# First transform stage with x as weights, and its result turned by DMA transposes inside SBUF

## The chip, the cores and the metric

The kernel runs on one core of one Trainium2 chip. The metric is the device time of one execution in microseconds (us), lower is better. Before the change it is 745.37 us, the median of three runs (744.99 to 745.52).

## The reference

The input is mixed along the sequence by a filter in the frequency domain, and a two-layer network with a leaky ReLU follows:

```python
# x: (8, 3008, 256); filt_r, filt_i: (1505, 256); w_in: (256, 2048); w_out: (2048, 256), all float32
X = np.fft.rfft(x, axis=1)
Y = X * (filt_r + 1j * filt_i)[None, :, :]
y = np.fft.irfft(Y, n=3008, axis=1).reshape(24064, 256)
h = y @ w_in
out = np.maximum(0.01 * h, h) @ w_out
```

## The kernel before

**The transform.** The length 3008 is split as 94 x 32. A batch goes through four stages, each of them matmuls with constant matrices, in half precision with sums in single precision:

1. Stage 1 (`s1_group`, L257) transforms along the 94 (on the partitions of `x_sb`, 32 blocks of 256 channels). The constant `fwd1` is the weights, x moves past it: one matmul of 512 columns for two blocks, 16 groups per batch. The result has the 96 used frequency rows (four parts of 32 rows, 24 of them used) on the partitions. It is copied to half precision in `st1`, and for every second group stored to the DRAM scratch `dz1` (L267).
2. The next transform runs along the 32, so the 32 must come to the partitions. `t1_load` (L274) reads `dz1` back in the other order into `z1`, six loads of 256 KB per batch; `z1` is a ring of four places, a half of `big[1]`. Stage 2 (`s2_group`, L311) has 12 groups of two matmuls with the constant `f2_sb`. VectorE multiplies with the filter (L320, L323), SyncE's queue swaps real and imaginary halves from `p2` to `p3` (L321, L322), GpSimd adds (L326).
3. Stage 3 (`sa_group`, L333) goes back along the 32. ScalarE copies to `st2`, which is stored to a second scratch `dz2` (L337).
4. Stage 4 (`sb_group`, L358) loads `dz2` in the other order into `z2` (L281) and takes that data as weights: four matmuls with 128x128 of data as weights and 94 columns of the constant `i1_sb` moving. The copy to `yt` (L347) reads its bank with a stride.

The first batch (b = 0) goes another way, by VectorE transposes, and is written out by hand in the string `FIRST`; it is not part of the change, which is for batches 1 to 7.

**The network.** The 24064 tokens are taken in 47 chunks of 512: `moe1` (L524) multiplies with `w_in`, ScalarE applies the leaky ReLU (L527), and `products` (L597) multiplies with `w_out` by seven products of half size, from sums and differences that VectorE makes (L563); the first chunks do it plainly (L689). Results leave by stores on SyncE's queue (L583).

**The order of work.** All instructions are put in order at build time. A list `work` holds steps with a planned time, in units of which a chunk has 8 (`SL`); the transform of a later batch is woven between the matmuls of earlier chunks. From the plans of two batches that are 47 units apart and lie 88 us apart in the order of PE's work, a unit is about 1.88 us. `PLANS` holds for each batch the time and step of the stages (first use of stage 1 and step, of stage 2 and step, the lag of stage 3, stage 4 and step, and the offset and step of the x loads for the next batch). `load_time` (L736) places the loads of `z1` and `z2`: at `LEAD` before the first use, but not before the last group of the stage before, plus an allowance (`LANDED`), and a group is planned no earlier than `READ` after its load. These numbers set only the order on each engine's list and queue; on the chip, semaphores make each instruction wait for its data.

**Queues.** SyncE (SP) issues the scratch stores and loads, the swaps and the output stores, in one list in order. GpSimd (POOL) issues the loads of x, and they stand in one list with its additions.

## Time and profile before

| | before |
|---|---|
| median of three runs | 745.37 us (744.99 to 745.52) |
| profiled execution: time / span | 744.82 / 742.8 us |
| PE (TensorE matmul) busy | 735.8 us, 99% |
| ACT (ScalarE) busy | 559.8 us, 75% |
| DVE (VectorE) busy | 506.7 us, 68% |
| POOL (GpSimd) busy | 167.6 us, 23% |
| granted TensorE clock | 0.999 |
| bytes moved by DMA | 113.84 MB, mean 153 GB/s |

The profile is of one execution. Shares are of its span; the rest of its time lies before the first and after the last instruction. PE are matmuls, PEld the weight loads, which run beside them. Lines such as L262 are lines of the kernel before; `out<-in` are the program's tiles with their numbers left out (`big`, `pf` for a bank of the sums, `dz` for the scratch). In the list of waits each line gives who waited, for whom, and in total, times and longest in us. In a timeline each line gives start, duration in us, engine, line, and how many instructions are merged. The end of a matmul is modelled, so what it occupies is read from one start to the next.

### The profile page before, as it was taken

The page shows a single profiled execution, that of the slowest core. Times are in us where ns is not written, and L with a number is a line of the kernel's source. Part 1 is how long each engine was busy: PE and PEld are TensorE (multiplying, and loading weights), DVE is VectorE, ACT ScalarE, POOL GpSimd, SP SyncE. Part 2 cuts the span into 40 slices and gives each one's busy share as a digit, 9 for nine tenths or more (in the row PEclk, how much of TensorE's full clock was granted, in tenths as well). Part 3 has the DMA queues.
Part 4 walks back from the last instruction along what each step waited for, and adds up shares of the span by engine and source line. Part 5 has one row for each costly group of instructions (what it writes and reads, how often), then busy time and mean ns, then how long its engine had stood idle before and what let it go on. Part 6 is the DMA issues. An engine that isn't in the chain of part 4 may idle for free.

```text
span 742.8 us, 18986 instructions
## 1 busy us (share of the span) xinstructions
PE 735.8 (99%) x7793; PEld 513.7 (69%) x7793; DVE 506.7 (68%) x690; ACT 559.8 (75%) x769; POOL 167.6 (23%) x171
## 2 busy tenths in 40 slices
PE   9999999999999999999999999999999999999997
PEld 3656667776777777777777777777777777777776
DVE  7987647776776766766777667766677676465566
ACT  4776797888878788877787787887777777777762
POOL 5503422332323212131232322121212210000000
PEclk9999999999999999999999999999999999999999
DMA  9997797888876666665676656544453343211012
GB/s 206 229 227 193 201 227 222 198 208 207 215 182 149 159 188 176 161 150 159 195 175 155 160 156 175 157 140 111 143 170 110 107 107 97 62 54 55 30 45 71
DMA packets 119879, 113.84 MB, mean 153 GB/s; under 512 B 16384, under 2 KB 93056, under 8 KB 119600
## 3 DMA queue, kind: packets, MB, share of 16 engines
q1 hardware_dynamic: 104457, 94.94, 43.9%
q0 software_dynamic: 15056, 17.50, 15.7%
q8 instruction: 61, 1.00, 0.6%
q10 hardware_dynamic: 279, 0.19, 0.1%
q14 instruction: 26, 0.21, 0.1%
HBM read 57.74 MB, written 50.33 MB: 145 GB/s over the span
## 4 chain that ended last, share of the span: by engine, by line
PE 98%; DVE 1%; ACT 0%; issue 0%; DVEq 0%; ACTq 0%
PE ph L524 44%; PE pf L597 18%; PE po_ps L597 18%; PE pf L262 3%; PE pf L358 3%; PE pf L311 2%; PE pf L333 2%; PE po_ps L380 2%; PE pf L689 1%; PE po_ps L689 1%; PE pf L432 0%; ACT yt L347 0%; PE pf L449 0%; PE ph L408 0%; DVE big L291 0%; DVE big L441 0%
## 5 line engine op out<-in xcount | busy, mean ns | idle before, releaser
L527 ACT ACTIVATE gt_c<-ph 128x1024 f16<-128x1024 f32 x376 | 385.6, 1026 | 131.6 <-PE ph L524 121.2
L524 PE MATMUL ph<-yt,w_in_sb 128*128 128x512 f16 x1504 | 446.9, 379 | 0.2 <-ACT yt L347 0.2
L597 PEld LDWEIGHTS <-gt_c 128*128 128x128 f16 x2800 | 203.3, 98 | 102.3
L326 POOL TENSOR_TENSOR y_b_g<-p_b_g,p_b_g 128x512 f16<-128x512 f32 x84 | 117.8, 1405 | 411.0 <-DMA p_b_g<-p_b_g 219.9
L597 PEld LDWEIGHTS <-big 128*128 128x128 f16 x2128 | 152.0, 98 | 69.2
L524 PEld LDWEIGHTS <-w_in_sb 128*128 128x128 f16 x1504 | 119.8, 98 | 12.9 <-DVE yt L347 0.4
L320 DVE TENSOR_TENSOR p_b_g<-pf,fb_sb 128x512 f32<-128x512 f32 x78 | 53.7, 688 | 31.4 <-PE pf L311 16.5
L597 PE MATMUL po_ps<-wt_sb,gt_c 128*128 128x128 f16 x704 | 70.0, 219 | 0.0
L597 PE MATMUL pf<-wt_sb,gt_c 128*128 128x128 f16 x688 | 68.5, 219 | 0.0
L597 PE MATMUL pf<-w_out_sb,gt_c 128*128 128x128 f16 x720 | 67.9, 219 | 0.0
L597 PE MATMUL pf<-wt_sb,big 128*128 128x128 f16 x704 | 67.2, 219 | 0.0
L597 PE MATMUL po_ps<-w_out_sb,gt_c 128*128 128x128 f16 x688 | 66.0, 219 | 0.0
L265 ACT CAST big<-pf 128x512 f16<-128x512 f32 x98 | 57.1, 588 | 11.7 <-PE pf L262 10.4
L597 PE MATMUL po_ps<-wt_sb,big 128*128 128x128 f16 x688 | 65.4, 219 | 0.0
L347 ACT CAST yt<-pf 128x376 f16<-128x376 f32 (+7 forms) x134 | 57.1, 441 | 10.0 <-PE pf L358 7.5
L563 DVE TENSOR_TENSOR big<-gt_c 128x2048 f16<-128x2048 f16 (+1 forms) x46 | 57.3, 1247 | 0.1
L323 DVE TENSOR_TENSOR p_b_g<-pf,fa_sb 128x512 f32<-128x512 f32 x84 | 57.2, 681 | 0.2
L563 DVE TENSOR_TENSOR big<-gt_c,big 128x2048 f16<-128x2048 f16 (+1 forms) x45 | 56.7, 1261 | 0.0
L563 DVE TENSOR_TENSOR gt_c<-gt_c 128x2048 f16<-128x2048 f16 x43 | 55.9, 1301 | 1.0
L563 DVE TENSOR_TENSOR big<-big,gt_c 128x2048 f16<-128x2048 f16 (+1 forms) x45 | 54.8, 1219 | 0.1
L335 ACT CAST big<-pf 128x512 f16<-128x512 f32 x84 | 49.0, 584 | 4.7 <-PE pf L333 2.7
L262 PE MATMUL pf<-x_sb,small_sb 128*128 128x512 f16 x109 | 41.3, 379 | 0.0
(98 smaller groups left out, 628.3 us busy)
## 6 DMA issues: line engine op xcount, KB each, us to landing
dz<-big SPq DMA_DIRECT2D x98, 256.0 KB
p_b_g<-p_b_g SPq DMA_DIRECT2D x156, 128.0 KB
out_dram<-ost_c_h SPq DMA_DIRECT2D x118, 128.0 KB
big<-dz SPq DMA_DIRECT2D x42, 256.0 KB
big<-dz SPq DMA_DIRECT2D x56, 192.0 KB
x_sb<-in_x_dram POOLq DMA_DIRECT2D x40, 192.0 KB, 4.4
x_sb<-in_x_dram POOLq DMA_DIRECT2D x2, 768.0 KB, 9.2
w_in_sb<-in_moe_w_in_dram POOLq DMA_DIRECT2D x1, 1024.0 KB, 13.7
```

The lines of the kernel that those rows point to most:

```text
L262: nc.tensor.matmul(ps, fwd1, x_sb[:, ds(2 * g, 2), :], start=True, stop=True)
L265: copy(st[:, ds(2 * (g % 2), 2), :], ps)
L320: nc.vector.tensor_tensor(p2[:], ps, fb, AL.mult)
L323: nc.vector.tensor_tensor(p1[:], ps, fa, AL.mult)
L326: ("y", b, g), lambda: nc.gpsimd.tensor_tensor(y1[:], p1[:], p3[:], AL.add)))
L335: nc.scalar.copy(st2[h % 4][:, ds(2 * (g % 2), 2), :], ps)
L347: copy(yt[:, dt, ds(to, 4 * n)].rearrange("p (a c) -> p a c", c=4), v[:, ds(a, n)])
L358: nc.tensor.matmul(ps[:, j, :], z2[h % 4][:, j, ts(dt, P)], i1_sb[:, 4 * h + j, :N1], start=True, stop=True)
L524: nc.tensor.matmul(ph[:, j, :], w_in_sb[:, dt, ts(ct, P)], yt[:, dt, ds(ci * CH % RING, CH)], start=(dt == 0), stop=(dt == NDT - 1))
L527: nc.scalar.activation(gts[ci][:, ds(2 * g, 2), :], ph, AF.Lrelu)
L563: nc.vector.tensor_tensor(*(v[:, ds(c0, n)] for v in (o, i0, i1)), op)
L597: nc.tensor.matmul(of[t], a()[:, c, ts(t, P)], w[:, c, :], start=(c == 0), stop=(c == NCH - 1))
```

## The change

Stage 1 of batches 1 to 7 exchanges weights and moving data. A group now takes four blocks and 128 of the 256 channels: four matmuls, each with 128x128 of `x_sb` as weights and 96 columns of the constant `fwd1m` moving (the 96 used columns of `fwd1`, closed up). Channels come out on the partitions. The copy puts the group into `turn_in`, a buffer of 6144 elements per partition in the second half of `big[2]`, which is made longer for it (`st1` and the store go; `idle`, used at the start only, moves into the same space). `turn_in` is arranged so that a DMA transpose from SBUF to SBUF (128 x 1024 elements of two bytes, 256 KB, eight blocks of 128x128) gives one place of `z1`. There are six per batch, issued from SyncE where the loads from `dz1` stood. The rows of the result come out in the order in which the second constant `f2_sb` is first loaded, so the later load of a reordered copy of it (`fwd2t_const`, 768 KB, L726) goes. `dz1` goes too.

One buffer serves all batches, so stage 1 of a batch comes after the last transpose of the batch before. The plans change with it: stage 1 of batches 2 to 7 starts later and is closer together, stage 2 of batch 1 is planned at 12.3 instead of 12.95 units with a step of 1.05 instead of 0.9, and the x loads for the next batch are placed differently. Half of the copies of stage 1 in batch 2 go to VectorE instead of ScalarE.

```diff
+    fwd1m = np.zeros((P, P))
+    fwd1m[:, :NW] = fwd1.reshape(P, 4, Q)[:, :, :NC].reshape(P, NW)
+    small = np.stack([fwd1, inv2, inv2r, inv2i, fwd1m], axis=1)
...
+    TURN = 0.6
+    TURNED = 1.7
-    F2T = 3.24
-    LEAD = (3.85, 7.37)
+    LEAD = (2.3, 7.37)
...
     PLANS = (
-        (0.68, 0.31, 12.95, 0.9, 4.35, 38.33, 2.78, 7.78, 1.61),
-        (12.19, 1.53, 42.87, 2.62, 7.4, 85.59, 2.85, 16.13, 2.12),
-        (40.7, 1.73, 77.28, 3.57, 5.62, 130.03, 2.65, -0.23, 2.52),
-        (63.95, 2.85, 119.86, 3.87, 7.04, 177.42, 2.92, 12.93, 2.24),
+        (0.68, 0.31, 12.3, 1.05, 4.35, 38.33, 2.78, 7.78, 1.5),
+        (24.2, 0.8, 42.87, 2.62, 7.4, 85.59, 2.85, 6.4, 2.12),
+        (53.5, 1.35, 77.28, 3.57, 5.62, 130.03, 2.65, 0.8, 2.2),
+        (91.2, 1.6, 119.86, 3.87, 7.04, 177.42, 2.92, 0.8, 2.55),
     )
...
-    small_sb = cpool.tile([P, 4, P], FP16, name="small_sb")
+    small_sb = cpool.tile([P, 5, P], FP16, name="small_sb")
...
-    big = [cpool.tile([P, Q * D], FP16, name=f"big{i}") for i in range(3)]
+    HALF = Q * D // 2
+    big = [cpool.tile([P, Q * D + (HALF // 2 if i == 2 else 0)], FP16, name=f"big{i}") for i in range(3)]
+    idle = big[2][:, Q * D : Q * D + CH]
+    big[2], more = big[2][:, : Q * D], big[2]
...
-    dz1 = [drp.tile([N2, P, D], FP16, name=f"dz1_{i}") for i in range(2)]
...
-    st1, st2, st1_more = ring(big[2], 0), ring(big[2], 1), ring(big[1], 1)
+    st2 = ring(big[2], 0)
+
+    turn_in = more[:, HALF :].rearrange("p (k t q n) -> p k t q n", k=NC, t=2, q=4)
 
     def s1_group(b, g, copy):
+        h, dt = divmod(g, 2)
+
         def go():
-            ps = bank("pf", 2, D)
-            h = g // 2
-            need(("x", b, h if b > 1 else 0), *[("st1", b, h - 4)] * (h > 3 and b > 1))
-            nc.tensor.matmul(ps, fwd1, x_sb[:, ds(2 * g, 2), :], start=True, stop=True)
+            ps = bank("pf", 4, NW)
+            need(("x", b, h if b > 1 else 0), *[("z1", b - 1, 5)] * (b > 1))
+            for j in range(4):
+                nc.tensor.matmul(ps[:, j, :], x_sb[:, 4 * h + j, ts(dt, P)], fwd1m[:, :NW], start=True, stop=True)
+            copy(turn_in[:, :, dt, :, ds(4 * h, 4)], ps.rearrange("p n (q k) -> p k q n", q=4))
             issued.add(("s1", b, g))
-            st = st1[h % 4] if b > 1 or h < 4 else st1_more[h % 4]
-            copy(st[:, ds(2 * (g % 2), 2), :], ps)
-            if g % 2:
-                soon(AFTER[0], lambda: noted(("st1", b, h), lambda: nc.sync.dma_start(
-                    dz1[b % 2][ds(4 * h, 4)].rearrange("n p d -> p n d"), st)))
         return go
 
     def t1_load(b, c):
         def go():
-            need(*[("st1", b, h) for h in range(8)], *[("s2", b, 2 * c - 7)] * (c > 3))
-            nc.sync.dma_start(z1[c % 4], turned(dz1[b % 2], N2, c))
+            need(*[("s1", b, g) for g in range(16)], *[("s2", b, 2 * c - 7)] * (c > 3))
+            nc.sync.dma_start_transpose(z1[c % 4].rearrange("p n (t d) -> p (n t) d", t=2),
+                                        turn_in[:, ds(4 * c, 4)].rearrange("p k t q n -> p (k t q n)"))
             issued.add(("z1", b, c))
         return go
...
-            groups.append((s1 + s1_step * g, 1, b, g, s1_group(b, g, dve if b == 1 and g % 4 < 3 else act)))
+            groups.append((s1 + s1_step * g, 1, b, g, s1_group(b, g, dve if b == 1 and g % 4 < 3 or b == 2 and g % 2 else act)))
...
-    at(F2T, lambda: noted(("f2t",), lambda: nc.sync.dma_start(f2_sb[:], f2t_d.ap())))
...
             loads[stage, b, c] = t = max(first_use[stage, b] - LEAD[stage // 2], place.get((stage, c % 4), 0),
-                                         when[end] + AFTER[4 * (stage // 2)] + LANDED)
+                                         when[end] + (TURN if stage == 1 else AFTER[4] + LANDED))
...
-                behind += READ
+                behind += TURNED if stage == 2 else READ
```

More of the change, by code (lines that the diff above doesn't have):

```diff
@@ L67, in _build_np_constants @@
     inv2i = np.concatenate([inv2[64:], inv2[64:]], axis=0)
-    small = np.stack([fwd1, inv2, inv2r, inv2i], axis=1)
-    fwd2t = fwd2.reshape(4, Q, NC, P).transpose(1, 0, 2, 3).reshape(P, NC, P)
+    fwd1m = np.zeros((P, P))
+    fwd1m[:, :NW] = fwd1.reshape(P, 4, Q)[:, :, :NC].reshape(P, NW)
+    small = np.stack([fwd1, inv2, inv2r, inv2i, fwd1m], axis=1)
     inv1t = np.zeros((P, N2, NW))
@@ L73, in _build_np_constants @@
     fwd2 = fwd2.reshape(P, FP, NC // FP, P).transpose(1, 0, 2, 3)
-    return tuple(np.ascontiguousarray(t).astype(np.float16) for t in (fwd2, inv1, small, fwd2t, inv1t))
+    return tuple(np.ascontiguousarray(t).astype(np.float16) for t in (fwd2, inv1, small, inv1t))
 @with_exitstack
@@ L109 @@
     TWICE = (2.2, 2.35)
-    F2T = 3.24
-    LEAD = (3.85, 7.37)
+    LEAD = (2.3, 7.37)
     AFTER = (0.53, 0.8, 1.33, 3.17, 0.39, 0.52)
     PLANS = (
[4 rows of a table removed]
[4 rows of a table added]
     )
-    f2_np, i1_np, small_np, f2t_np, i1t_np = _build_np_constants(N)
+    f2_np, i1_np, small_np, i1t_np = _build_np_constants(N)
     f2_d = nc.inline_tensor(f2_np, name="fwd2_const")
@@ L125 @@
     small_d = nc.inline_tensor(small_np, name="small_const")
-    f2t_d = nc.inline_tensor(f2t_np, name="fwd2t_const")
     i1t_d = nc.inline_tensor(i1t_np, name="inv1t_const")
@@ L190 @@
     ctx.enter_context(tc.manual_schedule())
-    fwd1, inv2, inv2r, inv2i = (small_sb[:, i, :] for i in range(4))
+    fwd1, inv2, inv2r, inv2i, fwd1m = (small_sb[:, i, :] for i in range(5))
     DH = D // 2
@@ L229 @@
     nc.gpsimd.dma_start(w_in_sb[:], moe_w_in.rearrange("(dt p) c -> p dt c", p=P))
-    idle = cpool.tile([P, CH], FP16, name="idle")
-    nc.vector.memset(idle[:], 0.0)
+    nc.vector.memset(idle, 0.0)
     one = cpool.tile([1, 1], FP32, name="one")
@@ L307, in go @@
             ps = bank("pf", 2, D, 1.75 if b == 1 and g % 2 == EXG else 1.2)
-            need(("z1", b, g // 2), ("f2t",))
+            need(("z1", b, g // 2))
             issued.add(("s2", b, g))
@@ L379, in keep_warm @@
         for _ in range(n):
-            nc.tensor.matmul(po_ps.rearrange("p a d -> p (a d)"), idle[:, 0:P], idle[:],
+            nc.tensor.matmul(po_ps.rearrange("p a d -> p (a d)"), idle[:, 0:P], idle,
                              start=True, stop=True)
```

## The prediction

> **What bounds the kernel now.** I read the page first (busy time, the slices, the chain that ended last), then the waits of PE, then the groups by line, and last a few stretches of the timeline around the first stage and around the load of its turned result. From the page:
>
> ```profile
> span 742.8 us, 18986 instructions
> PE 735.8 (99%) x7793; PEld 513.7 (69%) x7793; DVE 506.7 (68%) x690; ACT 559.8 (75%) x769; POOL 167.6 (23%) x171
> PEclk9999999999999999999999999999999999999999
> DMA  9997797888876666665676656544453343211012
> PE 98%; DVE 1%; ACT 0%; issue 0%; DVEq 0%; ACTq 0%
> ```
>
> TensorE is busy for 735.8 of 742.8 us, the clock is granted in full, and the chain runs through PE for 98% of the span. "Busy" alone could hide gaps, since the ends of matmuls are modelled, so the waits of PE decide. They name only a few tenths of a microsecond after the start, 0.2 of it for the second stage (L311):
>
> ```profile
> PE po_ps L380 <- DVE one L234: 1.2, 1, 1.2
> PE ph L404 <- issue: 0.5, 1, 0.5
> PE pf L311 <- ACT big L265: 0.2, 1, 0.2
> ```
>
> So PE works through its list without pause, and a change is worth what it does to that list, plus any wait that it creates. In the groups by line the modelled durations overlap (a 512-column matmul is given 379 ns), so I take what a matmul occupies from the starts in the timeline, one quad of the last transform stage (L358) and one first-stage matmul (L262) among products:
>
> ```profile
> 304.98 0.33 PE L358 MATMUL pf<-i_sb,big 128*128 128x94 f16 x4
> 305.15 0.45 PE L597 MATMUL po_ps<-wt_sb,big 128*128 128x128 f16 x5
> ...
> 307.79 0.38 PE L262 MATMUL pf<-x_sb,small_sb 128*128 128x512 f16 x1
> 308.00 0.28 PE L597 MATMUL pf<-wt_sb,gt_c 128*128 128x128 f16 x2
> ```
>
> From start to next start the L262 matmul takes 0.21 us, and four L358 matmuls, each with new weights from data, 0.17 us. Over all rows of the timeline from 70 to 730 us the means are 0.2159 us for an L262 (92 of them) and 0.0408 us for an L358 (112 quads); a product matmul of 128 columns takes 0.0555.
>
> **The change, part by part.**
>
> *First stage, PE.* Removed: 7 batches x 16 groups = 112 matmuls of 512 columns, 112 x 0.2159 = 24.18 us. Added: 448 matmuls of 96 columns with x as weights. They have the form of L358 (128x128 weights from an SBUF tile of data, a constant of about 94 columns moving), so 0.0408 x 96/94 = 0.0417 each, 18.67 us. Net -5.51 us, all of it on the path. (Each group sends 384 columns instead of 512.)
>
> One rule of the Trainium skill speaks against this. "TensorE: Matmul & The Clock Gate", section "LDWEIGHTS (loading the stationary operand)", gives a weight load about its columns over 1.2 in ns, so an estimate of 107 ns for 128 columns; if each of the 448 matmuls were paced by it they would take 47.8 us, and the sum would be 23.6 us above before. The trace disagrees: with new weights for each, L358 goes at 40.8 ns and the products at 55.5. That page of the Trainium skill also says that loads are pulled ahead of running matmuls, and the two spacings agree.
>
> *Evacuation of the first stage.* Before, 112 copies of 128x512 (ACT 588 ns, DVE about 691). After, 92 copies of 128x384 on ACT and 20 on DVE; a copy of the same strided reading, L347 with 128x376, takes 441 ns on ACT and 538 on DVE, so about 0.45 and 0.55. ACT: 100 x 0.588 - 92 x 0.45 = 17 us less; DVE: 20 x 0.55 - 12 x 0.691 = 2.7 us more. ACT is 75% and DVE 68% busy, PE waits for neither beyond 0.2 us: nothing on the path. Were that cover gone, DVE's 2.7 us would be the price. The new copies write into one turning buffer, so a batch's first copy must wait for the last transposes of the batch before. By the order of PE's instructions in the changed kernel, with the durations above, that is tightest between batches 3 and 4: the group that frees it runs 5.95 us before the first new copy's matmul. Covered while a transpose lands within that time.
>
> *DRAM scratch.* 56 stores and 42 loads of 256 KB leave the queue of SP, and one load of 768 KB (the reordered second-stage matrix): 26.5 of 113.84 MB. No wait of PE ended on them, so this gives nothing by itself. The constant block grows by 32 KB and lies ahead of the early x on SP's queue; at the 220 GB/s of the first 35 us that is 0.15 us at most on the path, between 0 and 0.3 with a busy queue; I take 0.15.
>
> *x loads on POOL's queue.* Loads for the next batch now follow the first-stage groups by at least 3.3 us in the plan, where before one stood 19.16 us in POOL waiting for L262. The tightest use (batch 2) comes 8.3 us after its load's planned issue, and 192 KB land after 4.4 us (median). Nothing, with 3.9 us to spare.
>
> *42 DMA transposes on SP.* No row shows one. What they replace:
>
> ```profile
> 112.87 1.76 SPq L274 DMA_DIRECT2D big<-dz  x4
> ...
> 117.43 0.38 PE L311 MATMUL pf<-big,f_sb 128*128 128x256 f16 x2
> ```
>
> The four loads of 256 KB were issued from 112.87 us on, and the first was used at 117.43 without a wait: at most 4.56 us from issue to use. The stretch from 112 to 118 us moved 229 GB/s, so 256 KB cost the queue 1.14 us. Let T be what one transpose of 256 KB costs the queue (SP's issuing or the DMA engines, whichever is longer). Lower end: 1.1 us, this row. Upper end: the page's row for this queue (104457 packets at 43.9% of 16 engines over 742.8 us) makes a packet 50 ns; if turning cuts 256 KB into pieces of 32 bytes, 8192 packets over 16 engines cost 25.6 us; pieces of 256 bytes, 3.2 us. I take 1.1 to 1.8, since the loads of this very row have the same bytes, queue and destination.
>
> What T costs is a matter of the order. I add 0.9 us from the last first-stage matmul to issue (a copy of 0.45 to 0.55 and an issue of 0.42, as L274's), and 2.0 us of fixed delay (so that the row's 4.56 us hold a transfer of its size in a full queue). With the order of PE's instructions:
> - Batch 1: last first-stage matmul to first second-stage matmul is 4.76 us of PE work. 0.9 + T + 2.0 fits while T is below 1.86. Batches 2 to 7 have 8.86, 5.68, 8.36, 7.10, 9.07, 8.14.
> - Behind the four transposes SP also has output stores and the p2-to-p3 swaps, for which POOL's add and then the third stage's matmul (L333) wait. In batch 3 that matmul comes 13.1 us after the last first-stage one, and 0.9 + 4T + 0.6 (issue) + 2.0 + 1.4 (POOL's add, 1405 ns) must fit: T below 2.05. In batch 1 group 1's swap has five transposes ahead and 17.05 us: T below 2.43.
> - Output stores rotate over four tiles, two per chunk of 15 us: a delay of 4T is covered.
>
> At T = 1.15 all of it fits, cost nothing; at 1.8 still nothing. At 2.5 batch 1 loses 0.6 and batch 3 1.8 us; at 3.0, 2.9 and 3.8 us. These two grow by 5 and 4 us per us of T, so the gain of 5.36 is used up at 9T - 20.35 = 5.36, T = 2.86 us. At 4 the other batches join, 18 us in all.
>
> *Sum*, on the profiled execution (744.82 us, span 742.8 and 2.0 around it): 744.82 - 24.18 + 18.67 + 0.15 = 739.46. That execution lies 0.55 under the median of the three runs, 745.37, so I predict 740.0.
>
> **The rivals.**
> - *A transpose costs 2 to 2.8 us.* For: nothing shows its price, and the margins in batches 1 and 3 end at 1.9 and 2.1. Against: 1.14 for a plain transfer. At 2.5: 740.0 + 2.4 = 742.4.
> - *Slower: the transposes are the new wait.* From T = 2.86 on, the second stage's matmul waits for its transpose and the third stage's for the swap queued behind it; at 3.2 (256-byte pieces) the stalls are 3.9 + 4.6 = 8.5 us, 748.5; at 4, 758. For: a turned write has small pieces, and small packets are dear on this queue. Against: the DMA engines lose the scratch traffic in just those stretches, and the transpose has one trip where store and load were two.
> - *Weights bind.* If each load of 98 ns (the weight rows of L358) were paid in full, 448 x 0.098 - 24.18 = 19.7 us more: 759.7. Against it stands the same group of L358, which is not so paced.
> - *No change*: the 5.5 us are eaten by chance by the stalls, T within 0.15 us of 2.86, or come back as waits in the start, where the first chunk's deadlines are tight: 745.
>
> **How the numbers follow.** Forecast 0.63 (own range 738.8 to 741), middle rival 0.13, slower by transposes 0.17, weights 0.02, no change 0.05. A measurement of this kernel tells about 0.2% (1.5 us) from no change. Faster: 0.63 + 0.13 + a little of the rest, less the edge of the middle rival, 0.75; same 0.06; slower 0.19. The range from 738.5 to 746.0 holds the forecast, the middle rival, no change and the nearest of the slow case, some 0.82.
>
> **What would show it.** L262's successor at 448 matmuls, four within 0.17 us in the timeline; PE's busy time some 5 us lower and the span with it; ACT some 17 us lower; bytes down to about 98 MB, the transposes' included; and PE's waits still without a line for the second stage (transpose) or the third (y). If instead the waits show PE at the second-stage line in batches 1 and 3 for whole microseconds, ended by a DMA into big, or at the third stage by POOL, T was above 2 and I am wrong by that sum; if the quads take over 0.3 us, the first term is wrong.

## The result: slower, 751.87 us against 745.15

The changed kernel takes 751.87 us (median of 6 runs, 748.7 to 752.87) where the kernel before takes 745.15 (744.12 to 745.52): a ratio of 1.0082, 95% interval 1.0061 to 1.0103. 740.0 was forecast, and a range of 738.5 to 746.0. The profiled execution is one of its shorter ones, 749.57 us, 4.75 above that of before; what follows is read from it, and the further 2.3 us up to the median have no profile of their own.

From the page of the changed kernel, the lines that answer to those of before, and the one of the packets:

```profile
span 747.8 us, 19535 instructions
PE 732.2 (98%) x8129; PEld 522.1 (70%) x8129; DVE 509.4 (68%) x698; ACT 547.6 (73%) x761; POOL 166.9 (22%) x171
...
PEclk9999999999999999999999999999999999999999
DMA  9977767775975488455964658543664343211012
...
DMA packets 128473, 98.43 MB, mean 132 GB/s; under 512 B 59153, under 2 KB 107153, under 8 KB 128193
...
PE 90%; DMA 4%; DVE 2%; ACT 2%; issue 1%; POOL 0%; SPq 0%; DVEq 0%; ACTq 0%; POOLq 0%
```

The clock is still granted in full, PE is busy 3.6 us less, and the span is 5 us longer: the matmuls take less time, and PE now waits. The chain that ended last, 98% PE before, is 90% PE, and DMA, VectorE and ScalarE have taken the rest. Bytes fell as worked out, to 98.43 MB, but packets under 512 B rose from 16384 to 59153: 42769 more, 1018 for each transpose of 256 KB, so they are of about 256 B (the packets of the trace show 43008 of exactly 256 B on this queue, 1024 for each, and a few hundred fewer of another kind).

The waits of PE after the change (who waited, for whom: total, times, longest, in us):

```profile
PE pf L314 <- DMA big<-big: 2.5, 3, 1.6
PE ph L389 <- ACT x_sb L476: 2.1, 1, 2.1
...
PE pf L314 <- DVE yt L350: 1.1, 1, 1.1
PE pf L336 <- POOL y_b_g L329: 0.6, 1, 0.6
...
PE pf L361 <- DVE p_b_g L326: 0.5, 1, 0.5
PE pf L314 <- ACT big L338: 0.4, 1, 0.4
PE pf L268 <- ACT big L338: 0.4, 1, 0.4
PE pf L361 <- ACT big L269: 0.4, 1, 0.4
```

L314 is the second stage (L311 before), L336 the third, L361 the fourth, L268 the first. The second stage waits for the transposes, but also for VectorE and ScalarE, and the other lines are new too. (L389 lies at 8.85 us, in the start.) The first-stage quads themselves are as forecast; in the timeline of PE a quad and its successor:

```profile
304.15 0.33 PE L268 MATMUL pf<-small_sb,x_sb 128*128 128x96 f16 x4
304.32 0.50 PE L600 MATMUL po_ps<-w_out_sb,gt_c 128*128 128x128 f16 x6
```

0.17 us for four, and 0.0421 us per matmul as the mean of 96 quads (forecast 0.0417).

To count the waits that are too short to be listed I laid PE's order, with each matmul at its spacing in the timeline, beside the actual starts of the 1504 matmuls of L527 (a drift of 0.057 us per chunk, which all these kernels have alike, is taken off). Before, PE loses 1.60 us between the first and the last of them; after, 10.61. The sum then closes: 24.18 us of old first stage against 448 x 0.0421 = 18.86 gives -5.32, the first network matmul starts 0.94 us later (35.62 for 34.68), waits grow by 9.01, together +4.63 of the +4.75 seen. By chunk of the network the waits lie at 50 to 95 us (the chunks with batch 1's second and third stage, 4.1 us where before has 1.3), at 120 us (batch 2's second stage, 1.75), at 144 to 150 (0.8), at 199 (batch 3's third stage, 1.0), at 232 (0.7) and at 535 (0.7); the rest is in pieces of 0.2.

### The profile page after: what moved, and what is told of

It reads as the page before. It is cut to its first block, busy times and chain, and to the rows that moved or that the text cites. A ratio compares the mean times of both kernels' runs of the same rounds, so it can differ in the third digit from the quotient of the medians.

```text
span 747.8 us, 19535 instructions
## 1 busy us (share of the span) xinstructions
PE 732.2 (98%) x8129; PEld 522.1 (70%) x8129; DVE 509.4 (68%) x698; ACT 547.6 (73%) x761; POOL 166.9 (22%) x171
## 2 busy tenths in 40 slices
DMA packets 128473, 98.43 MB, mean 132 GB/s; under 512 B 59153, under 2 KB 107153, under 8 KB 128193
## 4 chain that ended last, share of the span: by engine, by line
PE 90%; DMA 4%; DVE 2%; ACT 2%; issue 1%; POOL 0%; SPq 0%; DVEq 0%; ACTq 0%; POOLq 0%
PE ph L527 41%; PE pf L600 17%; PE po_ps L600 17%; DMA big<-big 3%; PE pf L361 3%; PE pf L268 2%; PE pf L314 2%; PE pf L336 2%; PE po_ps L692 1%; PE pf L692 1%; DMA big<-in_x_dram 1%; ACT gt_c L530 1%; PE po_ps L383 1%; DVE p_b_g L326 1%; DMA p_b_g<-p_b_g 1%
## 5 line engine op out<-in xcount | busy, mean ns | idle before, releaser
L527 PE MATMUL ph<-yt,w_in_sb 128*128 128x512 f16 x1504 | 447.1, 379 | 0.2 <-ACT yt L350 0.2
L527 PEld LDWEIGHTS <-w_in_sb 128*128 128x128 f16 x1504 | 118.0, 98 | 6.2 <-DVE yt L350 0.4
L566 DVE TENSOR_TENSOR big<-big,gt_c 128x2048 f16<-128x2048 f16 (+1 forms) x45 | 56.7, 1260 | 0.1
L338 ACT CAST big<-pf 128x512 f16<-128x512 f32 x84 | 49.1, 585 | 8.2 <-PE pf L336 6.8
L269 ACT CAST big<-pf 128x384 f16<-128x384 f32 x90 | 42.9, 477 | 11.2 <-PE pf L268 8.0
L361 PE MATMUL pf<-i_sb,big 128*128 128x94 f16 x448 | 37.0, 206 | 1.0 <-DVE p_b_g L326 0.5
## 6 DMA issues: line engine op xcount, KB each, us to landing
w_out_sb<-in_moe_w_out_dram POOLq DMA_DIRECT2D x1, 1024.0 KB, 13.9
```

What stands on the lines that cost most here:

```text
L269: copy(turn_in[:, :, dt, :, ds(4 * h, 4)], ps.rearrange("p n (q k) -> p k q n", q=4))
L338: nc.scalar.copy(st2[h % 4][:, ds(2 * (g % 2), 2), :], ps)
L361: nc.tensor.matmul(ps[:, j, :], z2[h % 4][:, j, ts(dt, P)], i1_sb[:, 4 * h + j, :N1], start=True, stop=True)
L527: nc.tensor.matmul(ph[:, j, :], w_in_sb[:, dt, ts(ct, P)], yt[:, dt, ds(ci * CH % RING, CH)], start=(dt == 0), stop=(dt == NDT - 1))
L566: nc.vector.tensor_tensor(*(v[:, ds(c0, n)] for v in (o, i0, i1)), op)
```

## The experiments

**Without the transposes.** The 42 transposes are left out.

```diff
-            nc.sync.dma_start_transpose(z1[c % 4].rearrange("p n (t d) -> p (n t) d", t=2),
-                                        turn_in[:, ds(4 * c, 4)].rearrange("p k t q n -> p (k t q n)"))
```

> The changed kernel without its 42 DMA transposes (stage 2 multiplies what lies in z1, so the output is wrong); all else, the order too, is kept. Three theories for the 12 us that the forecast missed (751.9 against 740.0). Order: a transpose costs the queue about what was forecast (1.25 to 1.55 us on SP), but the transposes come late, behind other entries of SP's list, and land later than 2.0 us after that, and PE, ACT and POOL wait for them. Turning: transposes hold up the other traffic on the DMA engines wherever they stand. Form: stage 1's new form costs by itself (448 weight loads, strided copies, VectorE's share). Order and turning: the waits go, 745.2 - 5.4 for PE + 0.9 for the later start + about 1 for waits on VectorE in batch 1 = 741 to 742. Form: above 745.

743.62 us, ratio 0.9975 (0.9961 to 0.9988). So the transposes cost 8.2 us, but without any of them a part of the gain is missing too: 5.3 us were to go, and 1.5 to 2 go. The waits beyond the order are 5.95 us in its profile, 4.35 more than before, 2.2 of it in the chunks from 50 to 95 us and 1.1 around 231 us:

```profile
PE pf L312 <- DVE yt L348: 1.1, 1, 1.1
PE pf L359 <- DVE p_b_g L324: 0.9, 1, 0.9
...
PE pf L312 <- ACT big L336: 0.4, 1, 0.4
PE pf L268 <- ACT big L336: 0.4, 1, 0.4
```

(Here L312 is the second stage, L359 the fourth, L268 the first.) These are waits for VectorE and ScalarE, not for a transfer.

**Plain copies in their place.** Each transpose becomes a copy of the same 256 KB, not turned.

```diff
-            nc.sync.dma_start_transpose(z1[c % 4].rearrange("p n (t d) -> p (n t) d", t=2),
+            nc.sync.dma_start(z1[c % 4].rearrange("p n d -> p (n d)"),
                                         turn_in[:, ds(4 * c, 4)].rearrange("p k t q n -> p (k t q n)"))
```

> Each transpose replaced by a plain copy of the same 256 KB from turn_in to the same place of z1, at the same place in SP's list (not turned, so the output is wrong). Order: the plain copies stand as late and the waits stay for the most part, with SP held 0.4 instead of 1.3 us for each: 746 to 750. Turning: as without transposes, 741 to 743.

745.44 us, ratio 1.0004 (0.9992 to 1.0016). A transfer in this place costs about 2 us, and that it turns, 6.4 by the medians and 5.8 by the ratios. In what way, two things can be read. The first is SP's time. The source view of the changed kernel for L276 (count, then shortest, median and longest in ns):

```profile
L276 SPq DMA_TRANSPOSE big<-big x42: 1249/1326/2969, 51.1 to 558.6; - x42
```

The same view of before gives 327, 431 and 601 ns for L274. The second is the DMA engines. Two windows, around the first four transposes of batch 1 and of batch 2, changed kernel (stretch, length, busy time of the five engines, granted clock, DMA share, GB/s):

```profile
50.50:58.00 7.50, 7.09 (x55) 4.74 (x54) 6.78 (x12) 3.63 (x5) 0.00 (x0) 1.00 0.83 128
116.50:123.00 6.50, 4.91 (x56) 3.47 (x53) 4.36 (x7) 3.00 (x5) 0.00 (x0) 1.00 0.80 167
```

and the same two with plain copies:

```profile
50.50:58.00 7.50, 7.17 (x56) 4.75 (x55) 6.82 (x13) 3.77 (x5) 0.00 (x0) 1.00 0.49 177
116.50:123.00 6.50, 5.76 (x65) 4.08 (x63) 5.19 (x7) 3.77 (x6) 0.00 (x0) 1.00 0.74 255
```

GB/s over share is what the engines move when all are busy: 154 and 209 with transposes, 361 and 345 with plain copies. So 256 KB turned take 1.25 to 1.7 us of all sixteen engines, plain 0.73 to 0.76. This is an estimate: the rows hold a little other traffic, and some rows of these profiles show shares above 1, so the times of packets overlap. The pages have the whole of SP's queue (bytes in MB, share of the span of sixteen engines), in this order for the kernel before, without transposes, with plain copies, and changed:

```profile
q1 hardware_dynamic: 104457, 94.94, 43.9%
q1 hardware_dynamic: 68697, 68.49, 32.2%
q1 hardware_dynamic: 74745, 79.50, 36.1%
q1 hardware_dynamic: 113049, 79.51, 41.3%
```

Times the spans of 742.8, 741.9, 745.8 and 747.8 us that is 326.1, 238.9, 269.2 and 308.8 us of all sixteen engines, so 1.66 us for one of the 42 transposes and 0.72 for a plain copy, which agrees. SP is held 5.44 us by batch 2's four transposes and 2.54 by its four plain copies. Both prices are about twice the plain one.

**SP's time or the engines'?** Two kernels keep the packets plain and hold SP longer, by two and by three copies for each transpose.

```diff
-            nc.sync.dma_start_transpose(z1[c % 4].rearrange("p n (t d) -> p (n t) d", t=2),
-                                        turn_in[:, ds(4 * c, 4)].rearrange("p k t q n -> p (k t q n)"))
+            for lo in (0, 512):
+                nc.sync.dma_start(z1[c % 4].rearrange("p n d -> p (n d)")[:, ds(lo, 512)],
+                                  turn_in[:, ds(4 * c, 4)].rearrange("p k t q n -> p (k t q n)")[:, ds(lo, 512)])
```

> Each transpose is two plain copies of 512 columns, which hold SP 2 x 0.64 = 1.28 us, next to the transposes' 1.33; the second stage multiplies what is not turned. Theory A (SP's hold): 749 to 751 us, and half-way between one plain copy (745.4) and three (753.7). Theory B (landing of turned packets): 745.4 to 747 us, the three copies' time being that of their longer hold alone.

and with `for lo, cnt in ((0, 352), (352, 352), (704, 320))` in the same lines:

> Each transpose is a plain copy of the same 256 KB at the same place of SP's list, cut into three DMAs of 352, 352 and 320 columns, so that SP is held for about 3 x 0.43 = 1.3 us, as by a transpose (1.33 us median), while the DMA engines move plain packets. The second stage multiplies what is not turned. One plain copy gave 745.4 us, the transposes 751.9. Theory A (SP's hold of 1.3 us per transpose delays the entries behind it): the time rises to 750 to 752 us and the first matmul of batch 2's and batch 3's second stage waits as after the change, 1.6 us in the profile's row of L314 behind a DMA. Theory B (what costs is how long a turned transfer takes until it has landed, 3 to 6.5 us): the time stays at 745 to 746.5 us, and PE waits for stage 2 less than 1 us in all behind DMAs.

Two copies: 746.96 us, ratio 1.0018 (1.0003 to 1.0033). Three: 753.7, 1.0104 (1.008 to 1.0128). Batch 2's first four buffers hold SP for 2.54 us as four plain copies, 5.10 as eight, 7.68 as twelve, and 5.44 as transposes. So a hold of nearly the transposes' length with plain packets costs 0 to 3 us over the one plain copy (the intervals touch), where the transposes cost 6.4. By the medians three quarters of their price is not SP's hold, at the edge of the intervals about half; what differs then, beside 0.34 us of hold, is that the packets on the engines are turned. One profile of each points the same way: from the first to the last network matmul 697.58 us pass with one copy, 696.50 with two, 699.61 with transposes. But the hold isn't harmless. With half as much again the time is as high as with transposes (703.94 in the profile), by a longer list alone, since the queue takes the engines no longer (36.4% of the span on the page, 36.2% with two copies). PE's waits with three copies (L337 is the third stage, L362 the fourth):

```profile
PE pf L337 <- POOL y_b_g L330: 3.5, 4, 2.2
...
PE pf L362 <- DMA big<-dz: 1.9, 2, 1.5
```

What suffers there is not the second stage but what stands behind on SP's list, the swaps and the loads for the fourth stage. Neither theory was right alone.

**The transposes from ACT's queue.** First as it is, then with the transposes of batches 2 to 7 planned apart (the plan of the run "issued one by one" further down).

```diff
-            nc.sync.dma_start_transpose(z1[c % 4].rearrange("p n (t d) -> p (n t) d", t=2),
+            nc.scalar.dma_start_transpose(z1[c % 4].rearrange("p n (t d) -> p (n t) d", t=2),
```

> The 42 transposes are issued from ACT's queue, not SP's; nothing else is changed. Theory A (they wait behind earlier entries of SP's list, 7.3 us in batch 2 behind the second-stage load and three output stores, and hold the swaps up behind them): the transposes are issued within 1 to 2 us of their last copy, batch 2's wait of 1.6 us and batch 3's of 0.6 us at the third stage go, and the time falls by 2.5 to 4 us, to 748 to 749 us. Theory B (the landing of turned transfers alone): issue moves, landing of 3.3 to 6.5 us stays, and the time falls by less than 1 us. Rival C: ACT, held 1.3 us by each issue, evicts and gives gelu later, and PE waits for ACT instead: 42 x 1.3 = 55 us of ACT's 547 busy, in which some waits of 0.5 to 1 us arise; the time stays at 751 or rises to 754 us.

> As the run before it, and the second stage is planned later behind the first: the transposes of batches 2 to 6 are due 4 units of the plan apart, with a lead of 5 in place of 2.3. By theory A the lead buys nothing beyond the queue and the time is that of the run before it within 1 us; by theory B it covers the landing, and the time falls to 746 to 748 us. By both, batch 1's part of about 4.3 us, which is there without any transpose, stays.

786.17 us (ratio 1.0533, 1.0499 to 1.0568) and 765.3 (1.0258, 1.0222 to 1.0294). The third possibility was right and priced far too low. ACT's timeline in the first of them:

```profile
49.70 6.96 ACTq L276 DMA_TRANSPOSE big<-big  x4
56.71 1.94 ACT L530 ACTIVATE gt_c<-ph 128x1024 f16<-128x1024 f32 x2 [7.04 <-issue]
```

Four transposes hold ACT for 7 us, two leaky ReLUs come late, and in every batch PE has one wait of 2.7 to 6.3 us for ScalarE. A long wait also costs more than its length. Behind the one of 4.98 us that ends at 57.79, the granted clock is 0.64 in the stretch from 60 to 65 us, where it was 1.00 from 45 to 50.

Planned apart they cost less, and in the later batches PE's waits for ScalarE are 2 us at most. Batch 1's four stay together in that plan, and its wait stays, at 5.3 us.

**Swaps off SP's list.** The two DMAs between stage 2 and stage 3 go to POOL's queue; the transposes stay.

```diff
-                soon(AFTER[1], lambda: nc.sync.dma_start(p3[0:64], p2[64:P]))
-                soon(AFTER[1], lambda: nc.sync.dma_start(p3[64:P], p2[0:64]))
+                soon(AFTER[1], lambda: nc.gpsimd.dma_start(p3[0:64], p2[64:P]))
+                soon(AFTER[1], lambda: nc.gpsimd.dma_start(p3[64:P], p2[0:64]))
```

> The swaps of halves between stages 2 and 3 (two DMAs of each group) are issued from POOL's queue in place of SP's, so that no transpose stands ahead of them; the transposes stay on SP. Theory A (SP's list, held 1.33 us by each transpose, gives the swaps late): POOL's adds no longer wait for late swaps, the waits of PE for POOL (0.6 us in the profile of the changed kernel, up to 3.5 in other runs) go, transposes too come earlier since SP has 156 entries fewer, and the time falls by 1.5 to 3.5 us, to 748.5 to 750.5. Theory B (landing of the turned transfers): only what PE waits for stage 3 goes, under 1 us: 751 to 752. Rival C: POOL's adds wait for a landing and hold the next group's swap behind them, so that a new wait for stage 3 comes up: 752 to 755.

757.87 us, ratio 1.0139 (1.0099 to 1.018): worse than anything expected. Where batch 3's transposes are in flight, POOL's timeline:

```profile
190.12 0.53 POOL L203 DMA_DIRECT2D x_sb<-in_x_dram  x1
190.64 0.53 POOL L324 DMA_DIRECT2D p_b_g<-p_b_g  x1
191.17 0.52 POOL L325 DMA_DIRECT2D p_b_g<-p_b_g  x1
198.19 1.26 POOL L329 TENSOR_TENSOR y_b_g<-p_b_g,p_b_g 128x512 f16<-128x512 f32 x1 [6.50 <-DMA p_b_g<-p_b_g]
```

The swap is issued at once, no transpose stands ahead of it in its list, and it lands 6.5 us later, against a median of 3.5 for this form on the page of the same run. In that stretch the windows show the DMA engines full:

```profile
192.00:194.00 2.00, 1.73 (x20) 1.24 (x19) 1.38 (x3) 1.24 (x2) 0.00 (x0) 1.00 0.98 153
194.00:196.00 2.00, 0.00 (x0) 0.00 (x0) 0.24 (x1) 0.00 (x0) 0.00 (x0) 1.00 1.19 151
196.00:198.00 2.00, 0.00 (x0) 0.00 (x0) 0.00 (x0) 0.00 (x0) 0.00 (x0) 0.74 1.01 195
198.00:200.00 2.00, 0.50 (x2) 0.23 (x2) 0.00 (x0) 0.00 (x0) 1.81 (x3) 0.50 0.01 2
```

From 192 to 198 the share is 1.0 to 1.2 at 151 to 195 GB/s, PE stands still for 5.8 us, and behind the stall the granted clock is 0.50. So a place clear of the transposes in a list does not make a swap land early. But the list isn't innocent either: ahead of the swap on the same queue stands an x load of 192 KB (L203). By the packets of the trace, the load's run from 191.95 to 194.66 us, the swap's from 193.19 to 197.38, and turned ones until 197.18. Over the 156 swaps of this run the time from issue to landing has a median of 2.5 us (70 swaps) where neither went on meanwhile, 3.6 (23) with at least 100 turned packets in it, 3.8 (45) with at least 10 packets of POOL's loads, and 4.4 (18) with both. A swap is late by either, and in this kernel POOL's queue puts it behind loads where SP's put it behind transposes.

The Trainium skill ("DMA: Bandwidth & Descriptors", section "Rules for kernel authors") says that spreading DMAs over issuing engines does not help, since all run on the same 16 engines; by that rule this run could only save issue time, and the trace agrees: from 193.2 to 197.2 us the swap's packets and turned ones run side by side. Of the 6 us that this run is slower than the changed kernel, the 5.8 us wait is the greater part; how much of this landing is the load's and how much the transposes' is not shown.

**Batch 1's VectorE.** One copy to `yt`, that of batch 0 at 62.5 us, goes to ACT.

```diff
-        at(REST[g - 10], lambda g=g: late_sb(1, g - 8, (act, dve)[g % 2]))
+        at(REST[g - 10], lambda g=g: late_sb(1, g - 8, (act, dve)[g % 2 and g != 11]))
```

> One copy into yt (the late fourth-stage quad of batch 0 that is evicted at 62.5 us) goes from VectorE to ACT, which idles there from 61.25 to 63.92 us. Theory A (batch 1's second stage, 4 us earlier than before the change, meets a VectorE list without a gap, 55.85 to 62.5 us): VectorE's next product starts 0.54 us earlier, the wait of L314 for yt, 1.1 us, goes, and the time falls by 0.5 to 1.1 us, to about 751. Rival (the list is as long as it is, and the next wait takes its place): 751.9 again, within 0.4 us.

749.36 us, ratio 1.0051 (1.0035 to 1.0067), 2.5 us less by the medians (the two intervals touch). The same without any transpose:

> The changed kernel without its 42 transposes (the second stage multiplies what its buffers happen to hold), and the yt copy of batch 1 on ACT. Without transposes alone 743.6 us. If batch 1's VectorE list is a loss of its own, apart from the transposes, the same 1 to 2.3 us go as with them: 741.3 to 742.7 us. If the copy only mattered because the transposes made batch 1 late, 743.6 again within 0.5.

742.58 us, ratio 0.9955 (0.9936 to 0.9973), against 743.62 and 0.9975. Both pairs go the same way, but in each the intervals overlap. In both profiles the wait of 1.1 us is gone (the chunk's waits fall from 2.31 to 0.75 us with the transposes). Without transposes this is the whole difference: from the first to the last network matmul 693.66 us pass where it was 694.96. With them it is not, 699.97 us against 699.61, since the third stage of batch 3 now waits 2.3 us where it was 0.6:

```profile
PE pf L336 <- POOL y_b_g L329: 2.3, 1, 2.3
```

So batch 1's list on VectorE is a loss of its own, about 1.1 to 1.3 us in this one copy; that 2.5 us go with the transposes is the medians' alone, and this profile doesn't show it. VectorE's timeline of the changed kernel shows the list:

```profile
60.47 0.69 DVE L320 TENSOR_TENSOR p_b_g<-pf,fb_sb 64x512 f32<-64x512 f32 x1
61.18 0.68 DVE L321 TENSOR_TENSOR p_b_g<-pf,fb_sb 64x512 f32<-64x512 f32 x1
61.87 0.69 DVE L326 TENSOR_TENSOR p_b_g<-pf,fa_sb 128x512 f32<-128x512 f32 x1
62.48 0.54 DVE L350 CAST yt<-pf 128x376 f16<-128x376 f32 x1
63.49 0.69 DVE L323 TENSOR_TENSOR p_b_g<-pf,fb_sb 128x512 f32<-128x512 f32 x1 [0.47 <-PE pf L314]
```

No gap up to the copy (from 55.85 on), and PE, whose next second-stage matmul needs the bank of that copy, waits 1.09 us until 63.08. Before, the same copy is at 59.65, and ahead of it VectorE had been idle for 0.45 and for 2.85 us: the second stage of batch 1 began 4 us later then, after the way through DRAM.

**Moving the plan and the start.** The first of these only brings the 32 KB of `fwd1m` by a DMA of its own, later:

```diff
-    nc.sync.dma_start(small_sb[:], small_d.ap())
+    nc.sync.dma_start(small_sb[:, :4], small_d.ap()[:, :4])
+    nc.sync.dma_start(small_sb[:, 4], small_d.ap()[:, 4])
```

> The changed kernel, but the 32 KB of the new constant fwd1m come by a DMA of their own behind the early x on SP's queue. If the 32 KB ahead of the early x made the first real matmul 0.8 us later (8.85 against 8.05 us), the profile shows it back near 8.05 and the time is about 0.9 us under the changed kernel: 751.0. If the later start was chance: 751.9, and it starts anywhere.

753.67 us (1.0104, 1.0055 to 1.0154): nothing gained. The start differs from kernel to kernel by more than this constant could: the first network matmul lies between 34.07 and 37.38 us in the profiles of these kernels, and at 34.40 in the one without transposes, which has the same constant in the same load.

With that edit, an earlier issue of the transposes and other starts of the stages:

```diff
-    TURN = 0.6
-    TURNED = 1.7
+    TURN = 0.7
+    TURNED = 2.6
...
-    LEAD = (2.3, 7.37)
+    LEAD = (5, 7.37)
...
-        (0.68, 0.31, 12.3, 1.05, 4.35, 38.33, 2.78, 7.78, 1.5),
-        (24.2, 0.8, 42.87, 2.62, 7.4, 85.59, 2.85, 6.4, 2.12),
-        (53.5, 1.35, 77.28, 3.57, 5.62, 130.03, 2.65, 0.8, 2.2),
-        (91.2, 1.6, 119.86, 3.87, 7.04, 177.42, 2.92, 0.8, 2.55),
+        (0.68, 0.31, 13.0, 1.0, 4.35, 38.33, 2.78, 7.78, 1.5),
+        (22.5, 0.8, 42.87, 2.62, 7.4, 85.59, 2.85, 6.4, 2.12),
+        (55, 1.25, 79, 3.5, 6.6, 130.03, 2.65, 0.8, 2.2),
+        (93.2, 1.35, 119.86, 3.87, 7.04, 177.42, 2.92, 0.8, 2.55),
```

> The small constant late as in the run before, and a new plan: transposes placed up to 5 instead of 2.3 units before use and 2.6 instead of 1.7 units ahead of the first group, stage 2 of batch 1 at 13.0 and of batch 3 at 79 units, stage 3 of batch 3 one unit later, stage 1 of batches 3 to 7 a little later and closer. In batch 2 the transposes now stand ahead of the fifth load of z2 and of three output stores. Order: the waits at stage 2 and at batch 3's stage 3 mostly go, 741 to 743.5. Turning: at best the start's 0.9 us and a part of the rest, 747 or more. Form: no better than 749.

748.56 us (1.0049, 1.0029 to 1.007; the interval overlaps the changed kernel's). No wait behind a transpose is left in PE's list, and 4.1 us behind POOL's adds (the third stage) have come up, in a profiled execution that is the longest of the runs (752.04).

Batch 1's second stage moved alone, later and closer together:

```diff
-        (0.68, 0.31, 12.3, 1.05, 4.35, 38.33, 2.78, 7.78, 1.5),
+        (0.68, 0.31, 14.5, 0.7, 4.35, 38.33, 2.78, 7.78, 1.5),
```

> The changed kernel with one number pair of the plan changed: stage 2 of batch 1 at 14.5 units with a step of 0.7 instead of 12.3 with 1.05, so that its first group comes about where it came before the change (its loads held it to 14.9 there). Without transposes 4.1 us of waits were left in the first four chunks, against 1.6 before the change. If the early stage 2 meets VectorE's one-time work (the filter's copies, the last copies of batch 0), the waits of the first four chunks fall from 4.6 to about 2 us and the time to 749.3. If the new copies of stage 1 are their cause, nothing changes: 751.9.

751.9 us (1.0065, 1.0046 to 1.0084): no gain that can be told. The wait for VectorE moves and grows to 3.0 us; closer steps pack its list more.

The transposes issued one by one, four units apart (with the values of `TURN`, `TURNED` and `LEAD` above, `SPREAD = 4`, the first stages of batches 2 to 4 at 24.2, 55 and 92.5, and batch 3's second stage at 78.5), and then the same with batch 1's plan just shown and batch 2's second stage at 43.8:

```diff
-            loads[stage, b, c] = t = max(first_use[stage, b] - LEAD[stage // 2], place.get((stage, c % 4), 0),
+            loads[stage, b, c] = t = max(first_use[stage, b] - LEAD[stage // 2] + SPREAD * c * (stage == 1 and b > 1 and c < 4), place.get((stage, c % 4), 0),
```

> The changed kernel with the four first transposes of batches 2 to 7 spread, 4 units apart, from 5 instead of 2.3 units before the first use, and stage 1 of batches 3 to 7 placed as in the run with more lead. The swap of the first group then has one or two transposes ahead instead of four. Order: the waits of chunks 5 to 12 and 32 mostly go, those of batch 1 stay: 746 to 748. Turning: 749 or more.

> Both edits together, the spread transposes and the late stage 2 of batch 1, and stage 2 of batch 2 at 43.8 instead of 42.87 units. Order: 743 to 744.5, under the kernel before. Turning: 746.5 or more.

752.58 us (1.0067, 1.0046 to 1.0089) and 751.84 (1.0059, 1.0042 to 1.0076). No wait of PE behind a transpose is left in either, and the chunks from 50 to 95 us (6.6 and 4.7 us of waits) and the one at 190 us, with batch 3's third stage and a load for stage 4 (3.5 and 4.1), have taken their place.

Swaps on POOL's queue, the one copy on ACT, and the transposes of batches 2 to 7 apart, put together from the edits above:

> Swaps from POOL's queue, the yt copy on ACT, and the transposes of batches 2 to 7 issued one by one, 4 units of the plan apart and 5 units ahead of the second stage. If SP's list and the landing are what the transposes cost (theories A and B), the 4.7 us of their waits go and with them 1 us of batch 1's: 745 to 747 us, equal to the kernel before; if batch 1's VectorE list were the smaller part, 743 to 744.5. If POOL's list takes SP's place (rival C): 750 or more.

756.77 us (1.0149, 1.0118 to 1.0179): POOL's list gives 7.4 us of waits at the third stage, where it gave 6.1 alone.

Then the queues as in the changed kernel, the copy on ACT, and only the places where PE was seen to wait moved:

```diff
-        (24.2, 0.8, 42.87, 2.62, 7.4, 85.59, 2.85, 6.4, 2.12),
-        (53.5, 1.35, 77.28, 3.57, 5.62, 130.03, 2.65, 0.8, 2.2),
+        (24.2, 0.8, 43.87, 2.6, 7.4, 85.59, 2.85, 6.4, 2.12),
+        (54.3, 1.3, 78.3, 3.52, 6.5, 130.03, 2.65, 0.8, 2.2),
...
-            loads[stage, b, c] = t = max(first_use[stage, b] - LEAD[stage // 2], place.get((stage, c % 4), 0),
+            loads[stage, b, c] = t = max(first_use[stage, b] - LEAD[stage // 2] - (stage == 1 and b > 3), place.get((stage, c % 4), 0),
```

> Queues as in the changed kernel, the yt copy of batch 1 on ACT (749.4 us), and the plan moved at the places of the other waits: batch 2's second stage one unit later (wait of 1.6 us), batch 3's first stage 0.8 and its second stage 1 unit later and its third 0.9 further behind it (1.0 to 2.5 us), transposes of batches 4 to 7 one unit earlier (0.5 us). If those waits are what the changed kernel loses, 1.5 + 1 to 2.5 + 0.5 us go from 749.4: 745 to 746.5 us. If they come back elsewhere (the plan shifts a wait and does not remove it), 748.5 or more.

757.35 us (1.0147, 1.0119 to 1.0175). This plan was flawed: batch 4's transposes are placed ahead of batch 3's last second-stage group and fill the buffer it reads, and batch 2's loads for stage 4 came up to 4 us late, so 11 us are lost around 200 us. It shows only that batch 2's second stage no longer waits (0.13 us for 1.75). The same copy on ACT, with smaller steps of the plan and without the earlier transposes:

```diff
-        (24.2, 0.8, 42.87, 2.62, 7.4, 85.59, 2.85, 6.4, 2.12),
-        (53.5, 1.35, 77.28, 3.57, 5.62, 130.03, 2.65, 0.8, 2.2),
+        (24, 0.8, 43.4, 2.5, 7.2, 85.59, 2.85, 6.4, 2.12),
+        (54.2, 1.25, 77.3, 3.5, 6.9, 130.03, 2.65, 0.8, 2.2),
```

> Queues as in the changed kernel, the yt copy of batch 1 on ACT (749.4 us with that alone), batch 2's second stage half a unit later with a smaller step (its end where it was), batch 3's first stage 0.7 later with a smaller step, its third stage 1.3 units further behind the second. If the waits seen there are what is lost, batch 2's 1.7 us and batch 3's 1.0 to 2.5 us go: 746 to 747 us. If the plan shifts the waits and does not remove them, 748.5 or more.

748.38 us, ratio 1.0025 (1.001 to 1.0039). So 1.0082, 1.0051 and 1.0025 in turn: two thirds of the loss are taken away by the ratios, and the interval still lies above 1. Its profile does not show where the gain lies. It is of the longest of the 12 runs (750.24 us), and from the first to the last network matmul it takes 699.41 us, hardly less than the changed kernel's 699.61. Batch 2 waits 0.9 us there where it was 1.75, batch 3's third stage 1.5, and a landing that took long at 448 us costs 1.4: in this execution the waits moved more than they went.

**Transposes in the kernel before.** A transpose of 256 KB from a constant into a spare buffer behind each load of L274, the rest as before:

```diff
             nc.sync.dma_start(z1[c % 4], turned(dz1[b % 2], N2, c))
+            nc.sync.dma_start_transpose(spare_to.rearrange("p (n d) -> p n d", n=8), f2_sb[:, 0:8, :].rearrange("p n d -> p (n d)"))
```

> The kernel before, with one DMA transpose of 256 KB (from the constant f2_sb into a spare buffer that nobody reads) issued behind each of the 42 loads of z1; the result is right. Turning (a transpose holds up the other traffic wherever it stands): 6 us or so over before, as between plain copies and transposes, 751 to 753. Order (a transpose is 1.3 us of SP and some 1.5 us of the queue, which the old plan with its long leads has room for): 745.5 to 747.5, and the timeline shows what a transpose costs the entries behind it.

802.56 us, ratio 1.0736 (1.0708 to 1.0765). This one was made badly: all 42 write the same buffer, so each waits on SP until the one before has landed. Within a batch's first four they start 3.05 to 5.17 us apart, and these four, with the loads between them, keep SP for 11 to 13 us. It does not tell SP's time from the engines', but it shows the end of that road:

```profile
PE pf L335 <- POOL y_b_g L328: 42.0, 7, 7.9
```

Seven waits at the third stage, 6 us each on average: swaps that stand behind a held SP.

## Why the prediction was wrong

- *First stage on PE, -5.51 us*: right. 0.0421 us per matmul makes it -5.32. The rule of the Trainium skill that I had weighed ("TensorE: Matmul & The Clock Gate", section "LDWEIGHTS (loading the stationary operand)", by which I estimated 107 ns for each load) found no support here: the 448 matmuls with new weights go at 42 ns.
- *T, a transpose's price on the queue, 1.1 to 1.8 us*: right. Four in a row hold SP for 5.44 to 6.21 us, 1.36 to 1.55 each, and the engines pay 1.25 to 1.7. The pieces are of 256 bytes; for such I had 3.2 us as a possibility, at 50 ns for a packet, the mean of the queue, and by the packets of the trace one takes 24.6 ns, so 1024 on sixteen engines 1.57 us. The rival "slower by transposes" was given 0.17 because it was tied to T above 2.86; it came at half that T. What failed is the slack that T was compared with.
- *"0.9 us from the last first-stage matmul to issue"*: this step failed in batch 2. I looked at what stands behind the transposes on SP's list, and never at what stands ahead. SP's timeline of the changed kernel in batch 2 and, for the next point, in batch 3:

```profile
102.15 10.47 SPq L284 DMA_DIRECT2D big<-dz  x5
...
114.91 2.34 SPq L586 DMA_DIRECT2D out_dram<-ost_c_h  x3
117.29 5.44 SPq L276 DMA_TRANSPOSE big<-big  x4
...
186.46 5.63 SPq L276 DMA_TRANSPOSE big<-big  x4
192.18 0.65 SPq L340 DMA_DIRECT2D dz<-big  x1
192.95 0.47 SPq L324 DMA_DIRECT2D p_b_g<-p_b_g  x1
193.47 0.59 SPq L325 DMA_DIRECT2D p_b_g<-p_b_g  x1
```

  In batch 2 the last first-stage matmul ends at 110.1 us and its copy soon after, but a load for stage 4 that waits for PE until 112.12 and three output stores that wait for VectorE until 114.91 come first: 7.2 us instead of 0.9. The second stage had 8.86 us of PE's work to pass and needed 7.2 + 3.3; it waited 1.59.
- *"2.0 us of fixed delay"*: right for the first transpose where the engines are free (batch 2, issue to first use 3.3 us, forecast T + 2.0 = 3.4), short where they are not: 4.2 us in batch 1, which cost 0.41, and 6.55 for batch 2's last one, issued at 137.12, for which ScalarE's first copy of batch 3 waits 2.0 us. For the swap behind the transposes in batch 3 it failed plainly. My sum from the last first-stage matmul (it ends at 184.95) was 0.9 + 4 x 1.4 + 0.6 + 2.0 + 1.4 = 10.5 of 13.1 us. Measured: 1.5 to issue, 5.63 for four, 0.86 with a scratch store that I had left out, 4.6 from the swap's issue to its landing where I had 0.6 + 2.0, 1.3 for the add: 13.9, and PE waited 0.64. What the 4.6 are, the packets of the trace show: the last turned ones end at 195.13 us, the scratch store's run from 194.87 on, and the swap's own only from 195.63 to 196.62. It stands behind turned packets on its own queue; the run with the swaps on POOL's queue shows that another queue is no way around them.
- *"Against: the DMA engines lose the scratch traffic in just those stretches"*: failed. In bytes they do. In the engines' time a turned byte costs 1.7 to 2.3 plain ones, so a batch's six transposes take 7.5 to 10 us of the engines. On the pages the time of SP's queue falls from 326.1 to 308.8 us of all sixteen engines (above), 17.3 us in all and 2.5 a batch: 5%, where its bytes fall by 16%. Little of the engines' time is saved, and four of the transposes come in one burst behind the last copy.
- *Evacuation of the first stage, "nothing on the path"*: failed in batch 1, and is the term that I would now size first. I took VectorE's 68% and a price of 2.7 us if cover were gone. VectorE's busy time did grow by 2.7 (506.7 to 509.4), but the cover was gone in one stretch for another reason than the copies: batch 1's second stage comes 4 us earlier and meets filter products, one-time work of the start and a copy in an unbroken list. That the way through DRAM delayed this stage until VectorE was free was nowhere in my sum. The run without transposes has 4.35 us of such waits, half of them in batch 1's chunks, the rest at other places of the moved plan.
- *ACT's 17 us*: 12.2 measured (559.8 to 547.6); the strided copy takes 477 ns, not 450. Off the path as said.
- *Constants and x loads*: the 0.15 us of the 32 KB can't be told among starts that differ by 3 us, and POOL's loads cost nothing that was seen.

So the change saves 5.3 us of matmuls, gives about 4 back at VectorE and ScalarE, half of it in batch 1's chunks, and loses 8.2 by the transposes (the run without them). Of these 8.2 the two profiles show 4.65 as waits of PE from the first to the last network matmul: transposes that wait behind other entries of SP's list, and swaps and loads that land late behind them. Another 1.2 is the later start of the changed kernel's profile, which the transposes need not have caused, and for the 2.3 us by which its median lies above its profile no wait is shown. The best of the versions here with transposes, 748.4 us, is still slower than the kernel before; what could be had if they cost nothing is shown by 742.6.

## What to carry to other kernels

A transfer that replaces another is to be compared in the time of the DMA engines and in the time that the issuing engine is held, not in bytes, and its landing in the fullest stretch, not in the freest. When a step's issue is placed by an in-order list, read what stands ahead of it there as carefully as what stands behind. And when a detour is taken out, ask what the stage behind it will now run into: a share of 68% says nothing about the 7 us in which it all meets.

## What the runs showed of the hardware

- A DMA transpose of 256 KB in half precision inside SBUF is cut in 1024 packets of 256 B, holds the engine that issues it for 1.33 us (median; 0.43 for a load of the same size, 0.56 for a plain copy in its place), and moves 154 to 209 GB/s per full share of the sixteen DMA engines. "VectorE: DVE Perf Modes" of the Trainium skill, section "The three transpose paths", gives about 90% of the DMA bandwidth for this way; here it is 43% to 61% of what plain copies move in the same places (154 of 361 and 209 of 345 GB/s), and the measurement decides.
- Its landing takes from 3.05 us at most (the shortest distance in the run with idle transposes) to 6.55 (in traffic). A plain swap of 128 KB on POOL's queue lands after 2.5 us (median) with neither turned packets nor loads of its queue under way, 3.6 with the first, 3.8 with the second, 4.4 with both.
- Issued from ACT, four of them held ACT for 7 us in one batch: the engine's own work stands behind the issue.
- A long stall of PE lowers its granted clock behind it: 0.64 from 60 to 65 us after a stall of 4.98 us (transposes on ACT's queue), 0.50 from 198 to 200 us after one of 5.77 (swaps on POOL's queue), with 1.00 before both.
- In this kernel SP's hold costs little at first and then much: with plain packets, 2.5 us for a batch's four costs nothing against before, 5.1 us 0 to 2.5, and 7.7 us 6 to 9.5 (by the intervals).
